# Two layers of memory attention and gMLP on one core: row norms and output splits moved to the end of each attention step, and the weights of the prologue staged and split another way

## The chip, the cores and the metric

The kernel runs on one core of a Trainium2 chip. The metric is the device time of one execution in microseconds; several executions are taken and their median is compared. A core has five engines that run side by side and meet only at semaphores: PE (TensorE, matmuls), DVE (VectorE), ACT (ScalarE), POOL (GpSimd) and SP (SyncE, which here only issues DMAs). Each works its own instruction list strictly in order, so an instruction that waits holds back everything behind it on its engine.

## The reference

`x` is 2048 rows of 640. All matrices and `x` are f32.

```
A(x):  q, k, v = x@wq, x@wk, x@wv      # 32 heads of 20, four segments of 512 rows
       for each segment s:
         a_dot = softmax(q k^T * scale + causal mask) v
         a_mem = phi(q) M / (phi(q) z + 1e-6)        # phi(t) = t+1 if t>0 else exp(t)
         o     = g * a_mem + (1-g) * a_dot           # g = sigmoid(beta), one per head
         M, z += phi(k)^T v, sum of phi(k)
       return o @ wo
B(x):  z = gelu(x @ w_in);  z1, z2 = halves of z;  z2 = layernorm(z2)
       return (z1 * (w_sp @ z2 + b_sp)) @ w_out      # w_in 640x1728, w_sp 2048x2048
x = x + A(LN(x));  x = x + B(LN(x));  x = x + A(LN(x));  x = x + B(LN(x))
```

## The kernel before

**Splits.** Every f32 operand of a matmul becomes a high and a low f16 part, and three products stand for one. The pattern "ACT rounds to the high part, DVE or POOL subtracts to get the low part" comes back everywhere: for weights it is `split_scaled` (L81 on ACT, L82 on DVE, after a power-of-two scale `iv` that needs the largest absolute value of the whole weight), for the normed rows `split_t` (L320 on ACT, L321 on POOL, then the transposing DMA L322 into `xt`), for the exponentials `cast` (`PH` on ACT, L1328, and `PL` on POOL, L1332, two halves of 640 columns per head).

**Stages of a layer.** Attention (`Attention.run`), then phase 1b (the input product of the gMLP, tile by tile of 128 rows in the order 0, 8, 1, 9, ...), then phase 2 (the spatial product and the output product). Layer 0 also has a prologue: `prologue` loads wv, takes its largest value and splits it; `early()` in `run` norms the first four row tiles, runs the value products (`value`, L1052, tile `vps`) and, in between, `query_key_weights` takes the maxima of wq and wk (L225) and splits them; then come the products of the first units (`unit`, L1111, `kps` and `qps`).

**Attention in steps.** 64 pairs of heads (16 in each segment) are worked in steps `t`, five steps for two pairs. In a step PE makes logits twice: by queries (`mp`, whose row maxima DVE takes, L1316 and L1319, `mxs`) and by keys (`es`, exponentiated by ACT into `P` or `Pb`, L1293). `cast` splits them, `pvs` (L1366) multiplies by the values, `combine` (L1377 to L1394) divides and gates on DVE and POOL into `gm`; when a unit of six or eight heads is full, its `out` splits `gm` into `ohl` (L1402 on ACT, L1403 on POOL) and stores it. `by_queries`, `by_keys`, `pvs` are the rigid skeleton. Between them PE does the dense work: values, keys and queries of the next segment, the memory update (`mup` on PE; L1215 on DVE masks it into `mst`, and on POOL L1217 adds the old memory), the memory read (`num`, L1180, reads `mst`) and for some tiles the output projection (`yps`, L1084).

`prep(t)` makes a row tile's norm in two parts: `stats` (L305 to L308: mean and variance on DVE, the power on POOL, `lnrs`) and `norm` (L1033 on DVE, then the split). Such side jobs are put off with `post(k, f)`: `f` runs `k` steps later, in the list `self.later`, right after the step's logits and ahead of its `pvs` and `cast`. `self.half` runs at 0.8 of the step.

**What sets the order.** PE's order in the attention is the order in which this program is written. The other engines' order is found by a scheduler from priorities (`tc.high_priority`) and from explicit edges (`tc.issue_after`). SP's DMA queue has one order too, also by that scheduler.

**Start of phase 1b.** `load(t)` brings the row tile (L359) that the attention's projection has stored (L1092, `x<-xt`); `attn_out` norms it (`layernorm_stats`, then L390 and L391); `xn_t` splits it on ACT (L400) and DVE and transposes it by a DMA into `th` (L402), which the first matmul of phase 1b (`zp`, L412) reads.

Of the kernel before, what the change touches and what calls it, by code (L numbers as in the profile page):

```python
# [33 lines left out]
HP = 2000  # L34
# [147 lines left out]
def prologue(g, ctx, wv, wq, wk, wo, w_in, w_out):  # L182
# [7 lines left out]
    with tc.tile_pool(name="wpro", bufs=1, side="right", reuse_waits="tile") as p, \  # L190
# [5 lines left out]
        with tc.high_priority(offset=HP):  # L196
            am = p.tile([128, KD], F32, name="wamk")
            for k in range(KD):
                nc.vector.tensor_reduce(am[:, k:k + 1], st[:, k], AX.X, ALU.max, apply_absolute_value=True)
            nc.vector.tensor_reduce(g.wam[:, 0:1], am, AX.X, ALU.max)  # L200
            g.vscale = pow2_scales(g, p, pp, "wsc", g.wam, 0, 1)
        g.w["v"] = [wp.tile([128, KD, D], F16, name=f"wv{x}") for x in "hl"]
        g.wqk = {nm + x: nc.dram_tensor(f"w_{nm}{x}", (128, KD, D), F16, kind="Internal").ap() for nm in "qk" for x in "hl"}
        for k in range(KD):
            e = split_scaled(g, g.w["v"][0][:, k], g.w["v"][1][:, k], st[:, k], 0)
            if k == 2:
                g.third = e
    g.qk_w = wq, wk


def query_key_weights(g, stage, pool, psum, tag):

    nc, tc = g.nc, g.tc
    st = []
    for w, x in zip(g.qk_w, "hl"):
        parts = [g.top[1].tile([128, 2160], F32, tag=f"wi1{x}", name=f"wst{x}1")[:, :3 * D].rearrange("p (k c) -> p k c", c=D),
                 g.top[0].tile([128, 1600], F32, tag=f"wo{x}", name=f"wst{x}2")[:, :2 * D].rearrange("p (k c) -> p k c", c=D)]
        st.append([parts[k // 3][:, k % 3] for k in range(KD)])
        for k in range(KD):
            nc.sync.dma_start(st[-1][k], w[k * 128:(k + 1) * 128, :])  # L220
    for i, nm in ((1, "q"), (2, "k")):
        with tc.issue_after(g.vscale.ins):
            am = pool.tile([128, KD], F32, tag="wamk", name="wamk")
            for k in range(KD):
                nc.vector.tensor_reduce(am[:, k:k + 1], st[i - 1][k], AX.X, ALU.max, apply_absolute_value=True)  # L225
# [6 lines left out]
        for k in range(KD):  # L232
            split_scaled(g, h[:, k], l[:, k], st[i - 1][k], i)
        yield

# [102 lines left out]
def phase1b(g, o_d, x, x1_d, z1_d, zh, zl):  # L338

    nc, tc = g.nc, g.tc  # L340
    with ExitStack() as ctx:
# [75 lines left out]
        g.loaded, g.gelu, g.lo = {}, {}, {}  # L417
# [33 lines left out]
        with tc.high_priority(offset=3 * HP2):  # L451
            a = load(0)
        with tc.high_priority(offset=HP2):
            xn = attn_out(0, *a)
            a = load(ORDER[1])
            th = xn_t(*xn)
        for i, t in enumerate(ORDER):
# [3 lines left out]
            if i + 1 < NT:  # L461
                xn = attn_out(ORDER[i + 1], *a)
# [402 lines left out]
def attn_consts(g, cp, beta):  # L865
# [6 lines left out]
    with tc.tile_pool(name="tmp", bufs=1) as tp, tc.tile_pool(name="acp", bufs=1, space=PSUM) as pp:  # L872
        f = tp.tile([128, 192], F32, name="fmask")
        for t, n, b, sg, op in ((g.eye, 64, 0, 1, ALU.not_equal), (g.step["q"], 192, -64, 1, ALU.is_ge), (g.step["k"], 192, 64, -1, ALU.is_ge)):
            nc.vector.memset(f, 0.0)
            for h in range(2):
                v = f[64 * h:64 * h + 64, :n]
                nc.gpsimd.affine_select(v, v, [[sg, n]], op, BIG if op is ALU.not_equal else -BIG, base=b, channel_multiplier=-sg)
            nc.vector.tensor_copy(t, f[:, :n])
# [7 lines left out]
        nc.vector.tensor_scalar(g.gate, g.gate, 1.0, 0.125, ALU.add, ALU.mult)  # L887

# [29 lines left out]
class Attention:  # L918
# [9 lines left out]
    def __init__(self, g, x, o_d, x1_d):  # L928
# [8 lines left out]
        self.now, self.later, self.half, self.rd = None, {}, {}, set()  # L937
        self.lead = []

    def post(self, k, f, c=None, into=None):  # L940
# [7 lines left out]
        (self.later if into is None else into).setdefault(t, []).append(f)  # L948
# [60 lines left out]
    def prep(self, t):  # L1009
# [4 lines left out]
        nc.sync.dma_start(xt, self.x[t])  # L1014
        ln = []

        def behind():
            ctx = ExitStack()
            for e in (g.hold[:2] or (g.third,)) if t > 1 else ():
# [11 lines left out]
        def last():  # L1031
            mv, rs = ln
            nc.vector.tensor_scalar(xt, xt, mv[:, 0:1], rs, ALU.subtract, ALU.mult)  # L1033
            hl = self.e2.tile([128, 2, D], F16, tag="xh", name="xnhl")
            e = split_t(g, hl, self.xt[s % 2][:, :, :, c], xt, low=nc.vector if g.hold and t in (2, 3) else nc.gpsimd)
            if t == 3:
# [4 lines left out]
    def value(self, t):  # L1041
# [5 lines left out]
        for n in range(2):  # L1047
# [8 lines left out]
            def out(ps=ps.rearrange("p (h d) -> p h d", d=DH), v=self.vs[s % 2][:, t % 4, n * 16:(n + 1) * 16, :]):  # L1056
                nc.scalar.mul(v[:, :, 0:DH], ps, QS)
                nc.vector.scalar_tensor_tensor(v[:, :, DH + 1:], ps, QS, v[:, :, 0:DH], ALU.mult, ALU.subtract)
# [38 lines left out]
    def unit(self, s, m):  # L1097
# [3 lines left out]
        for nm in "qk" if s else "kq":  # L1101
# [96 lines left out]
    def update(self, s, m):  # L1198
# [20 lines left out]
        self.post(1, out)  # L1219

    def stack(self, nm, s, m, hl):
# [6 lines left out]
        if nm == ("k" if s else "q"):  # L1228
# [93 lines left out]
    def cast(self, n, h):  # L1322
# [7 lines left out]
        def low(engine):  # L1330
            for c in (slice(0, 640), slice(640, 1280))[::-1 if n % 2 and h else 1]:
                engine.tensor_tensor(PL[:, c], P[:, h, c], PH[:, c], ALU.subtract)  # L1332
# [20 lines left out]
    def pvs(self, n, h, s, m, h0):  # L1353
        nc = self.nc
        PH, PL = self.P.pop((n, h))
        if h == 0:
            pv = self.po.tile([128, 512], F32, tag="pv", name="pv")
# [318 lines left out]
```

## Time and profile before

| | |
|---|---|
| median of 3 runs | 2218.08 us (2214.55 to 2218.99) |
| the profiled execution, its own time | 2217.2 us |
| its span | 2215.5 us |
| mean granted TensorE clock | 0.991 |
| busy: PE / DVE / ACT / POOL | 2087.8 / 1625.6 / 1250.9 / 1402.7 us |
| prologue (to the first `mp`) | 0 to 66.8 us |
| attention, layer 0, without its end | 66.8 to 575 us |
| end of that attention, to the first `zp` | 575 to 594 us |
| attention, layer 1, without its end | 1130 to 1660 us |
| end of that attention, to the first `zp` | 1660 to 1677 us |

The stage borders are the starts of the named tiles' first matmuls in the timeline, rounded. A row of a timeline reads: start, length, engine, line, operation, output<-inputs, count, and in brackets the idle time of that engine before the row with what ended it. "(x30)" behind a busy time is a number of instructions.

### The profile page before, as it was taken

Reading aid. Unit: us, or ns where it says so; the run is one execution under the profiler, and the core shown is the slowest. Engines: PE = TensorE matmul, PEld = TensorE weight load, DVE = VectorE, ACT = ScalarE, POOL = GpSimd, SP = SyncE. Lnnn points to the kernel's source line nnn. Section 1 sums busy time; section 2 is a strip of 40 time slices with the busy share of each in tenths; the row PEclk is TensorE's granted clock in tenths of the full one; section 3 lists DMA queues with packets and bytes.
Section 4 is the critical chain, followed back from the end, with each engine's and each line's share of the span. In section 5 each row is a group of like instructions: output and inputs, shape, how many; then the busy total and the mean of one; then the engine's idle time right before and its main releaser. Section 6 shows DMA issues by size and latency. Waiting matters only on the chain.

```text
span 2215.5 us, 53079 instructions
## 1 busy us (share of the span) xinstructions
PE 2087.8 (94%) x21322; PEld 1265.2 (57%) x21322; DVE 1625.6 (73%) x2889; ACT 1250.9 (56%) x1641; POOL 1402.7 (63%) x1172
## 2 busy tenths in 40 slices
PE   5998888999899999999999989989999999999999
PEld 3555655666545555555555556656665555555555
DVE  7788788788587758888657787787875764675563
ACT  4588788788644433333326987878884433333331
POOL 3387898788645345566414889888894433674660
PEclk9999999999999999999999999999999999999999
DMA  6666557344776686666455456553455335876752
GB/s 177 163 174 184 133 163 197 96 121 126 185 199 182 162 278 171 170 183 178 137 167 131 112 139 153 126 118 90 123 141 145 106 110 185 217 175 171 177 142 82
DMA packets 537703, 342.79 MB, mean 155 GB/s; under 512 B 411600, under 2 KB 463312, under 8 KB 537456
## 3 DMA queue, kind: packets, MB, share of 16 engines
q1 hardware_dynamic: 537456, 339.39, 57.2%
q8 instruction: 167, 2.74, 0.5%
q14 instruction: 80, 0.66, 0.1%
HBM read 159.18 MB, written 92.55 MB: 114 GB/s over the span
## 4 chain that ended last, share of the span: by engine, by line
PE 67%; DVE 14%; ACT 7%; issue 4%; DMA 4%; POOL 3%; SPq 1%; ACTq 0%; DVEq 0%; POOLq 0%
PE ga L670 12%; PE zp L412 11%; PE cyp L706 7%; PE pv L1366 4%; PE qps L1111 4%; PE vps L1052 3%; PE gb L670 3%; PE mp L1255 3%; PE yps L1084 3%; DVE mxs L1319 3%; PE gc L670 3%; PE gd L670 3%; PE kps L1111 2%; PE es L1255 2%; ACT PH L1328 2%
## 5 line engine op out<-in xcount | busy, mean ns | idle before, releaser
L1332 POOL TENSOR_TENSOR PL<-P,PH 128x640 f16<-128x640 f32 x384 | 535.1, 1422 | 86.7 <-PE pv L1366 67.9
L1319 DVE TENSOR_REDUCE mxs<-mp 128x2 f32<-128x1024 f32 (+2 forms) x384 | 320.2, 861 | 123.4 <-PE mp L1246 121.3
L1293 ACT ACTIVATE P<-es,sc 128x1024 f32<-128x1024 f32 (+1 forms) x256 | 271.6, 1061 | 102.0 <-PE es L1246 95.8
L640 POOL TENSOR_TENSOR ts<-ts,wt 128x512 f32<-128x512 f32 x196 | 283.3, 1457 | 11.0
L412 PEld LDWEIGHTS <-th 128*128 128x128 f16 x1920 | 188.0, 98 | 169.6 <-issue 6.9
L1328 ACT CAST PH<-P 128x1280 f16<-128x1280 f32 x192 | 239.7, 1249 | 2.5 <-PE pv L1366 1.0
L670 PEld LDWEIGHTS <-wts 128*128 128x128 f16 x1536 | 150.2, 98 | 134.0 <-issue 5.5
L670 PE MATMUL ga<-zh,wts 128*128 128x432 f16 x768 | 210.8, 346 | 4.5 <-ACT u L737 4.5
L308 POOL TENSOR_TENSOR lnrs<-lnve,mhalf 128x1 f32<-128x1 f32 x96 | 59.8, 631 | 230.2 <-DVE lnve L307 223.1
L1332 POOL TENSOR_TENSOR PL<-Pb,PH 128x640 f16<-128x640 f32 x124 | 175.8, 1447 | 20.3 <-PE pv L1366 19.3
L412 PE MATMUL zp<-wi,th 128*128 128x432 f16 x960 | 181.2, 346 | 3.5 <-ACT z L448 3.5
L640 POOL TENSOR_TENSOR ts<-wt,wt 128x512 f32<-128x512 f16 x28 | 33.9, 1211 | 226.3 <-DMA wt<-wn 226.3
L1052 PE MATMUL vps<-wvh,xt 128*128 128x320 f16 x640 | 154.8, 309 | 23.7 <-DVE relu L1143 13.0
L670 PEld LDWEIGHTS <-wt 128*128 128x128 f16 x1152 | 112.7, 98 | 96.5
L1366 PE MATMUL pv<-vs,PH 128*128 128x41 f16 x2560 | 158.6, 182 | 8.6 <-DVE gm L1387 5.5
L706 PE MATMUL cyp<-wuh,ut 128*128 128x320 f16 (+1 forms) x896 | 163.6, 299 | 2.7 <-DMA ut<-un 1.8
L706 PEld LDWEIGHTS <-ut 128*128 128x128 f16 (+1 forms) x1344 | 131.1, 98 | 57.5 <-DMA ut<-un 4.0
L1255 PEld LDWEIGHTS <-qk 64*128 64x128 f16 (+1 forms) x2048 | 77.9, 94 | 150.1 <-issue 129.3
L1366 PE MATMUL pv<-vs,PL 128*128 128x41 f16 x2560 | 156.3, 181 | 2.6 <-POOL PL L1332 2.6
L412 PE MATMUL zp<-wi1h,th 128*128 128x432 f16 x640 | 149.9, 349 | 2.2 <-DMA th<-xnhl 2.1
L524 DVE SCALAR_TENSOR_TENSOR wn<-wr,wsc,wn 128x512 f16<-128x512 f32 x126 | 92.9, 775 | 76.8 <-ACT wn L523 76.7
L1366 PEld LDWEIGHTS <-PH 128*128 128x128 f16 x2560 | 138.6, 96 | 15.2 <-ACT xnhl L400 2.9
(224 smaller groups left out, 5286.5 us busy)
## 6 DMA issues: line engine op xcount, KB each, us to landing
qk<-st SPq DMA_DIRECT2D x256, 120.0 KB
wr<-in_B_w_sp_dram SPq DMA_DIRECT2D x60, 512.0 KB
z<-z SPq DMA_DIRECT2D x32, 432.0 KB
cz<-z SPq DMA_DIRECT2D x32, 432.0 KB
xt<-in_A_x_dram SPq DMA_DIRECT2D x32, 320.0 KB
st<-khl SPq DMA_DIRECT2D x40, 256.0 KB
st<-qhl SPq DMA_DIRECT2D x40, 256.0 KB
x<-x SPq DMA_DIRECT2D x32, 320.0 KB
```

The costliest lines, as they stand in the source:

```text
L412: nc.tensor.matmul(zp[:, n, :FHH], a[:, k, :], b[:, k, c:c + FHH], start=(k == 0 and j == 0), stop=(k == KD - 1 and j == 2))
L640: nc.gpsimd.tensor_tensor(t, a, t if b == "t" else get(b), ALU.add if op == "+" else ALU.subtract)
L670: nc.tensor.matmul(ps, w[:, a, k % 4, :], z[:, k, j, :], start=start and k == 0 and i == 0, stop=k == NP - 1 and i == 2, skip_group_check= ...
L706: nc.tensor.matmul(yp[:, n, :320], a[:kn[k], k, :], b[:kn[k], k, n * 320:(n + 1) * 320], start=(k == 0 and j == 0), stop=(k == KO - 1 and ...
L1052: nc.tensor.matmul(ps, a[:, k, c], b[:, k, n * 320:(n + 1) * 320], start=(i == 0), stop=(i == 14))
L1111: nc.tensor.matmul(ps, a[:, k, c], b[:, k, :], start=(i == 0), stop=(i == 14))
L1255: nc.tensor.matmul(out[:, h, o:o + w], a[r, ac], b[r, bc], start=o == 0, stop=False, skip_group_check=True)
L1293: g.exp = nc.scalar.activation(P, E, AF.Exp, scale=g.esc)
L1319: e = nc.vector.tensor_reduce(mx[:, :, n, j], mp[:, :, o:o + w], AX.X, ALU.max)
L1328: nc.scalar.copy(PH, P[:, h])
L1332: engine.tensor_tensor(PL[:, c], P[:, h, c], PH[:, c], ALU.subtract)
L1366: nc.tensor.matmul(pv[:, i, h, :41], x[:, c:c + 128], v[:, j, h0 + h, :], start=(j == 0 and x is PH), stop=(j == i and x is PL), skip_grou ...
```

## The change

1. *Prologue, staging.* The raw rows of wq and wk are loaded into the tiles that will later hold the exponentials (`Pf`, `Pb`) instead of the top tiles. wq's five loads are issued behind the second row tile's load and ahead of the first transposing DMA; wk's five after the row tile of t=3, still ahead of the third and fourth transposing DMA.
2. *Prologue, splits.* wv is split in ten pieces of 320 columns, all of the first half's before the second's. The ten maxima of wq and wk are tied each to one eviction of a value product (`g.vlow`) and to the end of wv's split. Of wq and wk only columns 0 to 255 go through `split_scaled`; the other 384 columns are scaled on POOL (`tensor_scalar`), rounded on ACT and subtracted on POOL, ten times each. The key mask and the gate constants move behind wv's scale (`late_consts`). The first unit makes queries before keys.
3. *Steps.* `stats`, `norm` and `combine`'s `out` go to a new list `self.end`, run after all else of the step; the memory update's DVE part goes to the front of its step's list (`first=True`).
4. *End of an attention.* Of the last pair's `PL`, POOL makes the first half of each head and DVE the second (before: POOL one head, DVE the other, two steps later). The `pv` PSUM tile of two of the last three pairs comes from the pool `pm`. `combine`'s first operation of the last but one pair waits for the last `PL`. Phase 1b's loads of tiles 0 and 8 are made at its start with high priority, their norms tied behind two late `combine`s (`g.near`).

The core of the diff:

```diff
-        for k in range(KD):
-            e = split_scaled(g, g.w["v"][0][:, k], g.w["v"][1][:, k], st[:, k], 0)
+        for n in range(2):
+            c = slice(n * 320, (n + 1) * 320)
+            for k in range(KD):
+                e = split_scaled(g, g.w["v"][0][:, k, c], g.w["v"][1][:, k, c], st[:, k, c], 0)
...
+def load_rows(g, i):
+    for k in range(KD):
+        g.nc.sync.dma_start(g.qk_raw[i][k], g.qk_w[i][k * 128:(k + 1) * 128, :])
...
     for i, nm in ((1, "q"), (2, "k")):
-        with tc.issue_after(g.vscale.ins):
+        with tc.issue_after(g.split.ins), tc.issue_after(g.normed[i + 1].ins):
             am = pool.tile([128, KD], F32, tag="wamk", name="wamk")
             for k in range(KD):
-                nc.vector.tensor_reduce(am[:, k:k + 1], st[i - 1][k], AX.X, ALU.max, apply_absolute_value=True)
+                with tc.issue_after(g.vlow[(KD * (i - 1) + k) // 2].ins):
+                    g.kmax = nc.vector.tensor_reduce(am[:, k:k + 1], st[i - 1][k], AX.X, ALU.max, apply_absolute_value=True)
...
         for k in range(KD):
-            split_scaled(g, h[:, k], l[:, k], st[i - 1][k], i)
+            split_scaled(g, h[:, k, first], l[:, k, first], st[i - 1][k][:, first], i)
         yield
+    for i, nm in ((1, "q"), (2, "k")):
+        h, l = g.w[nm]
+        for k in range(KD):
+            w = st[i - 1][k][:, rest]
+            nc.gpsimd.tensor_scalar(w, w, g.iv[:, i:i + 1], None, ALU.mult)
+            nc.scalar.copy(h[:, k, rest], w)
+            nc.gpsimd.tensor_tensor(l[:, k, rest], w, h[:, k, rest], ALU.subtract)
...
-        for nm in "qk" if s else "kq":
+        for nm in "qk" if s or m == 0 else "kq":
...
-        self.post(1, out)
+        self.post(1, out, first=True)
...
-        self.post(2, out)
+        self.post(2, out, into=self.end)
...
                     for d, f in zip((2, 4), self.prep(i)):
-                        self.post(d, f)
+                        self.post(d, f, into=self.end)
...
             with self.behind(DVE):
                 until(t + 1)
+            with self.behind(DVE):
+                for f in self.end.pop(t, ()):
+                    f()
...
-        if h == 0 or n < self.N - self.TAIL:
-            low(nc.gpsimd)
-        else:
-            self.post(2, lambda: low(nc.vector))
+        for i, c in enumerate((slice(0, 640), slice(640, 1280))[::-1 if n % 2 and h else 1]):
+            self.low = (nc.vector if i and n >= self.N - self.TAIL else nc.gpsimd).tensor_tensor(PL[:, c], P[:, h, c], PH[:, c], ALU.subtract)
...
+            p, tag = (self.pm, "ms") if n in (self.N - 3, self.N - 1) else (self.po, "pv")
...
+        two = [pe2.tile([128, D], F32, tag="x1", name="x1") for _ in range(2)]
+        with tc.high_priority(offset=HP):
+            for t, x1 in zip(ORDER, two):
+                g.loaded[t] = nc.sync.dma_start(x1, x1_d[t])
...
         with tc.high_priority(offset=HP2):
-            xn = attn_out(0, *a)
-            a = load(ORDER[1])
+            with tc.issue_after(g.near[-4].ins):
+                xn = attn_out(0, two[0])
```

The order of the instructions moves at many places; three of them follow.

**DVE, prologue.** The stretch behind wv's split: `vs` is the eviction of a value product (PE's next one needs it done), `wamk` a maximum over one raw tile of wq or wk, `xt<-xt` a row norm. Before:

```order
L305 BN_STATS lnst<-xt 128x6 x2
L307 TENSOR_SCALAR lnve<-lnmv 128x1
L306 BN_AGGR lnmv<-lnst 128x2
L307 TENSOR_SCALAR lnve<-lnmv 128x1
L1058 SCALAR_TENSOR_TENSOR vs_297<-vps,vs_297 128x16x20
L1033 TENSOR_SCALAR xt<-xt,lnmv,lnrs 128x640 x2
L225 TENSOR_REDUCE wamk<-wsth_452 128x1 x3
L1058 SCALAR_TENSOR_TENSOR vs_297<-vps,vs_297 128x16x20
L225 TENSOR_REDUCE wamk<-wsth_453 128x1 x2
L1058 SCALAR_TENSOR_TENSOR vs_297<-vps,vs_297 128x16x20
L226 TENSOR_REDUCE wam<-wamk 128x1
L225 TENSOR_REDUCE wamk<-wstl_459 128x1 x3
```

and now:

```order
L1098 SCALAR_TENSOR_TENSOR vs_312<-vps,vs_312 128x16x20
L238 TENSOR_REDUCE wamk<-P 128x1 x2
L1071 TENSOR_SCALAR xt<-xt,lnmv,lnrs 128x640
L1098 SCALAR_TENSOR_TENSOR vs_312<-vps,vs_312 128x16x20
L238 TENSOR_REDUCE wamk<-P 128x1 x2
L1098 SCALAR_TENSOR_TENSOR vs_312<-vps,vs_312 128x16x20
L238 TENSOR_REDUCE wamk<-P 128x1
L239 TENSOR_REDUCE wam<-wamk 128x1
L238 TENSOR_REDUCE wamk<-P 128x1
L1098 SCALAR_TENSOR_TENSOR vs_312<-vps,vs_312 128x16x20
L238 TENSOR_REDUCE wamk<-P 128x1 x2
L62 TENSOR_REDUCE wmx<-wtp 1x1
```

The maxima now stand at most two between two evictions, where there were three or five.

**DVE, a step of the second segment with a memory update.** `mst<-mup` is the memory that PE's `num` waits for, `khl` the low part of the keys. Before:

```order
L1316 TENSOR_REDUCE mxs_304<-mp 128x2x2
L305 BN_STATS lnst<-xt 128x6 x2
L1129 SCALAR_TENSOR_TENSOR khl<-kps,khl 128x512
L1215 TENSOR_TENSOR mst_305<-mup,bmask 128x168
L306 BN_AGGR lnmv<-lnst 128x2
L307 TENSOR_SCALAR lnve<-lnmv 128x1
```

and now:

```order
L1356 TENSOR_REDUCE mxs_319<-mp 128x2x2
L1255 TENSOR_TENSOR mst_320<-mup,bmask 128x168
L1169 SCALAR_TENSOR_TENSOR khl<-kps,khl 128x512
L326 BN_STATS lnst<-xt 128x6 x2
L327 BN_AGGR lnmv<-lnst 128x2
L328 TENSOR_SCALAR lnve<-lnmv 128x1
```

The memory goes from behind the statistics and the keys to the front, and the statistics go behind the keys.

**SP, the end of layer 0's attention.** `x_..<-x_0_8` is the load of tile 8's stored rows (L359 before, L373 and L385 now), `wst` the raw weights of w_in, `th` phase 1b's transposed tile. Before:

```order
L129 DMA wst<-in_B_w_in_dram 128x864 x4
L1076 DMA xt<-in_A_x_dram 128x640
L359 DMA x_11495<-x_0_8 128x640
L1406 DMA o_3<-ohl 128x4x120
L359 DMA x_11563<-x_0_1 128x640
L1067 DMA_TRANSPOSE o<-o_2 128x10x128
L1406 DMA o_3<-ohl 128x4x120
L1092 DMA x_0_9<-xt 128x640
L1076 DMA xt<-in_A_x_dram 128x640
L359 DMA x_11637<-x_0_9 128x640
L1092 DMA x_0_10<-xt 128x640
L402 DMA_TRANSPOSE th<-xnhl 128x10x128
```

and now:

```order
L373 DMA x_11504<-x_0_8 128x640
L1385 DMA qk_308<-mr 2x4x128
L129 DMA wst<-in_B_w_in_dram 128x864 x4
L1116 DMA xt<-in_A_x_dram 128x640
L1442 DMA o_3<-ohl 128x4x120
L1107 DMA_TRANSPOSE o<-o_2 128x10x128
L1132 DMA x_0_9<-xt 128x640
L1442 DMA o_3<-ohl 128x4x120
L1116 DMA xt<-in_A_x_dram 128x640
L385 DMA x_11604<-x_0_1 128x640
L1132 DMA x_0_10<-xt 128x640
L385 DMA x_11678<-x_0_9 128x640
```

with `th`'s first transposing DMA next. Tile 8's load has moved ahead of the four loads of w_in; the loads of tiles 1 and 9, whose buffers are free only once ACT has read tiles 0 and 8, now stand closely ahead of `th`'s transposition.

More of the change, by code (lines that the diff above doesn't have):

```diff
@@ L887, in attn_consts @@
         nc.vector.tensor_scalar(g.gate, g.gate, 1.0, 0.125, ALU.add, ALU.mult)
+def attn_consts(g, cp):
+    nc, tc = g.nc, g.tc
+    g.eye = cp.tile([128, 64], F16, name="eye")
+    g.step = {nm: cp.tile([128, 192], F16, name="step" + nm) for nm in "qk"}
+    with tc.tile_pool(name="tmp", bufs=1) as tp, tc.tile_pool(name="acp", bufs=1, space=PSUM) as pp:
+        f = tp.tile([128, 192], F32, name="fmask")
+        for t, n, b, sg, op in ((g.eye, 64, 0, 1, ALU.not_equal), (g.step["q"], 192, -64, 1, ALU.is_ge)):
+            step_mask(g, f, t, n, b, sg, op)
         row = tp.tile([1, 3, 128], F32, name="mrow")
@@ L936, in __init__, with post @@
         self.mem, self.last, self.stacked, self.waiting = False, -1, -1, False
-        self.now, self.later, self.half, self.rd = None, {}, {}, set()
+        self.now, self.later, self.half, self.end, self.rd = None, {}, {}, {}, set()
         self.lead = []
-    def post(self, k, f, c=None, into=None):
+        g.near, g.normed, g.vlow = {}, {}, {}
+    def post(self, k, f, c=None, into=None, first=False):
         if self.now is None:
@@ L947, in post @@
             t += 1
-        (self.later if into is None else into).setdefault(t, []).append(f)
+        todo = (self.later if into is None else into).setdefault(t, [])
+        todo.insert(0 if first else len(todo), f)
     @contextmanager
@@ L1013, in prep @@
         xt = self.e2.tile([128, D], F32, tag="xt", name="xt")
-        nc.sync.dma_start(xt, self.x[t])
+        with self.tc.high_priority(offset=HP) if t in (2, 3) and not g.wo.made else ExitStack(), \
+                self.tc.issue_after(self.second.ins) if t == 3 and not g.wo.made else ExitStack():
+            self.row = nc.sync.dma_start(xt, self.x[t])
         ln = []
@@ L1434, in early @@
                     yield w
-                    if t > 1 and i in AT:
+                    if t == 2 and i in AT:
                         next(weights, None)
-            for _ in weights:
-                pass
-            yield from self.unit(0, 0)
+            next(weights, None)
+            for i, w in enumerate(self.unit(0, 0)):
+                yield w
+                if i == 6:
+                    next(weights, None)
+                elif i == 20:
+                    for _ in weights:
+                        pass
         rd = [(G * s + RD[m] + 5 * (c0 > 0), s, m, c0) for s in range(1, nseg) for m in range(NU) for c0 in range(0, len(UH[m]), 6)]
@@ L1595, in run @@
                 until(t + 1)
+            with self.behind(DVE):
+                for f in self.end.pop(t, ()):
+                    f()
         assert not self.half
-        for t in sorted(self.later):
-            self.now = None
-            for f in self.later[t]:
-                f()
+        self.now = None
+        for left in (self.later, self.end):
+            for t in sorted(left):
+                for f in left[t]:
+                    f()
 def phase1a(g, x, o_d, x1_d, nseg=NSEG):
```

80 lines of the change are left out of this document (44 added, 36 removed).

## The prediction

> **What bounds the kernel now.** I read the page's first and fourth parts, then the table by stage, then PE's waits in each, then the other engines' rows ahead of the longest.
>
> ```profile
> PE 2087.8 (94%) x21322; PEld 1265.2 (57%) x21322; DVE 1625.6 (73%) x2889; ACT 1250.9 (56%) x1641; POOL 1402.7 (63%) x1172
> PE 67%; DVE 14%; ACT 7%; issue 4%; DMA 4%; POOL 3%; SPq 1%; ACTq 0%; DVEq 0%; POOLq 0%
> ```
>
> The chain of waits is two thirds PE. PE is idle for 2215.5 − 2087.8 = 127.7 us; the change removes no matmul, so that is all there is to win. The stage table says where it lies (columns: stage, length, busy of PE, PEld, DVE, ACT, POOL, clock, DMA share, GB/s):
>
> ```profile
> 0.00:66.80 66.80, 43.60 (x221) 24.00 (x223) 48.10 (x132) 27.57 (x44) 16.89 (x37) 0.92 0.63 180
> 66.80:575.00 508.20, 465.51 (x7172) 300.88 (x7172) 416.40 (x802) 414.68 (x504) 416.84 (x345) 0.98 0.56 150
> 575.00:594.00 19.00, 11.89 (x188) 8.74 (x186) 8.38 (x22) 9.27 (x11) 12.14 (x10) 0.94 0.89 189
> 1130.00:1660.00 530.00, 497.26 (x7383) 319.98 (x7382) 404.06 (x784) 417.48 (x511) 414.51 (x350) 0.99 0.51 130
> 1660.00:1677.00 17.00, 12.92 (x208) 9.41 (x206) 8.35 (x22) 10.62 (x11) 13.04 (x11) 1.00 0.48 137
> ```
>
> PE stands idle 23.2 us in the prologue, 42.7 and 32.7 in the two attentions, 7.1 and 4.1 at their ends: 109.8 of the 127.7, all in the stages that the change touches. In the attentions DVE, ACT and POOL are each busy near 80%: an instruction moved there makes room for one and delays another.
>
> **Prologue, what leaves.** PE's three waits after its first value product, then what the products between them ran at:
>
> ```profile
> 31.65 0.31 PE L1052 MATMUL vps<-wvh,xt 128*128 128x320 f16 x1 [2.59 <-DMA xt<-xnhl]
> 45.84 1.03 PE L1111 MATMUL kps<-xt,wkh 128*128 128x512 f16 x2 [3.14 <-ACT wkh L81]
> 47.94 0.61 PE L1111 MATMUL kps<-xt,wkl 128*128 128x512 f16 x1 [1.07 <-DVE wkl L82]
> 45.80:56.50 10.70, 9.45 (x30) 0.69 0.29 95
> 56.50:63.40 6.90, 6.63 (x30) 1.00 0.57 153
> 18.72 3.31 SPq L220 DMA_DIRECT2D wsth<-in_A_wq_dram  x5
> 25.81 4.95 SPq L322 DMA_TRANSPOSE xt<-xnhl  x2
> 11.61 1.47 SPq L322 DMA_TRANSPOSE xt<-xnhl  x1
> 16.36 0.42 PE L1052 MATMUL vps<-wvh,xt 128*128 128x320 f16 x1 [2.02 <-ACT wvh L81]
> 16.40:31.60 15.20, 10.66 (x60) 6.25 (x59) 15.06 (x29) 5.90 (x10) 4.16 (x5) 1.00 0.96 292
> 24.15 2.26 DVE L225 TENSOR_REDUCE wamk<-wsth 128x1 f32<-128x640 f32 x3
> 40.95 3.69 ACT L81 ACTIVATE wqh<-wsth,iv 128x640 f16<-128x640 f32 x5
> 47.01 1.68 DVE L82 SCALAR_TENSOR_TENSOR wkl<-wstl,iv,wkh 128x640 f16<-128x640 f32 x2
> 40.78 1.40 POOL L321 TENSOR_TENSOR xnhl<-xt,xnhl 128x640 f16<-128x640 f32 x1 [0.42 <-ACT xnhl L320]
> ```
>
> The third transposition is issued at 25.8 behind both weights' loads and lands for 31.65; in the new order wq's loads are long done by then, so the 2.6 go. The first unit's 30 products (15 of keys, 15 of queries; 45.8 to 56.5) take 10.7 us at a granted clock of 0.69, the second unit's 30 take 6.9 at 1.00: the first are fed by split pieces of 0.84 us of DVE (1.68 / 2) and 0.74 of ACT (3.69 / 5). With 256 columns instead of 640 a piece costs 40% of that, 0.34, less than three matmuls (6.9 / 30 × 3 = 0.69): 3.8 go, the 1.07 among them, and the 3.14 ahead of them with the five wk pieces no longer queued behind five wq pieces. Together 2.6 + 3.8 + 3.1 = 9.5 us.
>
> *What comes.* Ten maxima at 0.75 (2.26 / 3) stay, two at most between two evictions: where PE needs the eviction for its next product, up to 1.5 us is late. The first transposition, issued at 11.6, now finds five more loads of 320 KB ahead of it; at the 292 GB/s of the full stretch above they take 5.5 us, begun about 4 and so nearly through: a delay between 0 and 5.5, of which the wait for wv's split (to 16.36) covers the first part. POOL gets 20 operations of 384 columns. No row shows one; 640 columns take 1.40 (above), so 0.84 by columns, 1.40 as the upper end: 17 to 28 us, on an engine that is idle after 42.2 before. They start with the scale at about 40 and are done by 57, or by 68; the third unit's products are the first to read these columns, and they come behind two units of 6.9 us and a value product from about 44 on, so from 61. By the nearer end the cover holds. I take 3.5 us back out of the 9.5: **−6 us**, ends −10 and +1.
>
> The Trainium skill (DMA: Bandwidth & Descriptors, Queues, rings and completion order) says that each DMA engine takes descriptors in ring order, which speaks against wq's loads ahead of the first transposition. The trace agrees in kind: the third transposition above took 5.8 us to land behind loads. By that rule 3.6 MB (wv, wq, a row tile) would be drained at 292 GB/s first, near 14 us, and the first product would start some 2 us late: −4 instead of −6.
>
> **Steps, what leaves.** The memory read `num` waits for the memory behind other DVE work:
>
> ```profile
> 207.91 0.46 PE L1180 MATMUL num<-mst,phq 128*128 128x126 f32 x2 [1.51 <-DVE lnmv L306]
> 206.06 0.88 DVE L305 BATCH_NORM_STATS2 lnst<-xt 128x6 f32<-128x320 f32 x2
> 206.85 0.68 DVE L1129 SCALAR_TENSOR_TENSOR khl<-kps,khl 128x512 f16<-128x512 f32 x1
> 207.44 0.32 DVE L1215 TENSOR_TENSOR mst<-mup,bmask 128x168 f32<-128x168 f32 x1
> 384.01 0.77 PE L1180 MATMUL num<-mst,phq 128*128 128x126 f32 x2 [2.65 <-DVE lnmv L306]
> PE num L1180 <- DVE lnmv L306: 4.2, 2, 2.7
> PE num L1180 <- DVE mst L1215: 2.8, 4, 1.2
> ```
>
> `lnmv` is named as releaser, but 4.2 + 2.8 = 7.0 us a layer is one wait, for `mst`; layer 1 has the same two rows with the same sums. With `mst` first, the row at 207.91 loses 0.88 + 0.68, capped at its 1.51; the one at 384.01 has the statistics and two more pieces ahead and I give it 2.0; the four others have at most one such piece ahead and lose some 0.15 each. That is 4.1 a layer, 8.2 in all. The second wait is longer:
>
> ```profile
> 231.05 0.43 PE L1052 MATMUL vps<-wvh,xt 128*128 128x320 f16 x1 [4.90 <-DVE relu L1143]
> 226.88 0.72 ACT L320 CAST xnhl<-xt 128x640 f16<-128x640 f32 x1 [0.89 <-DVE xt L1033]
> 229.00 0.71 ACT L1402 CAST ohl<-gm 128x640 f16<-128x640 f32 x1
> 229.61 0.66 ACT L1138 ACTIVATE kps<-kps,sc 128x512 f32<-128x512 f32 x1
> PE vps L1052 <- DVE relu L1143: 6.9, 2, 4.9
> ```
>
> PE's value product waits for DVE's `relu`, that for ACT's `kps`, and ahead of it ACT has a norm's and an output's cast: with both behind, 0.72 + 0.71 = 1.4 us go, and the norm on DVE ahead of the keys makes it 2.4 in layer 0; in layer 1, where the same line's waits are shorter, I take 1.0. So 11.6 us could leave the steps.
>
> *What comes.* All moved work still runs, in the same step or the next; a step lasts about 508 / 160 = 3.2 us, so nothing is over 3.2 us later. Late next are the transposed rows, the stored outputs, and `mxs`, DVE's maxima that PE's next logits wait for, which the moved pieces now stand close ahead of. With DVE at 82% I give back two fifths (11.6 × 0.6): **−7 us**, ends −12 and 0.
>
> **Ends of the attentions.** DVE sits at 575 for tile 8's rows, and what is behind it waits in turn; the last pair's `PL` on DVE (2.77 us at 587.95) keep its last multiplication and PE waiting:
>
> ```profile
> DVE lnst L305 <- DMA x<-x: 4.7, 1, 4.7
> 582.63 0.40 PE L1255 MATMUL es<-qk 64*128 64x384 f16 x4 [2.45 <-ACT Pb L1293]
> PE pv L1366 <- DVE gm L1387: 2.6, 1, 2.6
> 587.95 2.77 DVE L1332 TENSOR_TENSOR PL<-Pb,PH 128x640 f16<-128x640 f32 x2
> 584.12 2.09 SPq L402 DMA_TRANSPOSE th<-xnhl  x1
> 590.93 0.83 ACT L400 ACTIVATE xnhl<-xn,lnrs 128x640 f16<-128x640 f32 x1 [3.68 <-DMA th<-xnhl]
> ```
>
> Without the load's delay and with the second PSUM tile, PE's 2.45 and 2.6 go, 5.0 us of layer 0's 7.1. But `th`, which the next stage's first matmul reads, now stands in SP's queue behind the load of tile 9, which waits for ACT to have read tile 8 (after the last `PH`, some 1.5 us later than 584.12), and it took until 590.9 to land. So I keep half: −2.5, and −0.5 in layer 1, whose end has 4.1 us of idle: **−3 us**, ends −6 and 0. The order of PE's products within layer 0's phase 1b moves too, with the same products; PE is the engine it runs on without a break, so I cost it at nothing, with ±2 for the range.
>
> **Sum.** −6 − 7 − 3 = −16 against the profiled execution's 2217.2, whose span is 1.7 less and which stands 0.9 under the median: 2201.2, or 2202 against the median.
>
> **Rivals.** *A, the steps give all back.* What DVE and ACT do later in a step takes `mxs`' and `es`' time, as 80% busy engines would; then only prologue and ends gain, 2218 − 9 = 2209. For it: DVE is busy 416.4 of 508.2 us, so there are few holes to move work into. Against it: `num` and `relu` are single waits with the causes named.
>
> *B, POOL's pieces are slow.* At the 1.40 us of a 640-column piece, POOL ends at 68 while the third unit's low parts are wanted from 61 on: PE waits 7, the prologue gains nothing (−6 + 7), the time is 2218 − 9 = 2209. The Trainium skill (GPSIMD Engine Reference, Elementwise — side-by-side cycle accounting) gives 4497 ns for 2048 f32 columns of a two-input operation against DVE's 2293; that is 0.84 for 384, an estimate from that page, and by it the splits are done in time and the sum stays at 2202. No row of this trace has 384 columns.
>
> *C, outputs late, slower than before.* A unit's split now follows the step's work, and the projection reads all units of a segment. This row shows that one place has no slack:
>
> ```profile
> PE vps L1052 <- DMA o<-ohl: 1.3, 1, 1.3
> ```
>
> Each layer has four segments. If each now waits a full step, 3.2 us, 8 × 3.2 = 26 us come on top of −16: 2228. Slower from 2.6 us a place (8 × 2.6 = 21, past the 16 and the 0.2%). Against it: POOL's order keeps `ohl` within one pair of `PL` of its old place.
>
> *D, all of it.* Everything named leaves and nothing comes back: 9.5 + 11.6 + 5.5 = 27, so 2191. For it: no new wait is certain; against it: the three busy engines.
>
> **Chances.** My sum 0.50 (2195 to 2208), A 0.15, B 0.08, C 0.10, D 0.10; 0.07 for no change, if PE's idle time only moves. The range 2190 to 2216 leaves C and that case out. A run tells 0.2% (4.4 us) from no change: faster 0.81 (of A's and B's 0.23 a little falls within), same 0.09, slower 0.10.
>
> **What would show it.** Right: the first `mp` near 61 instead of 66.8; `num` without `lnmv` among its waits and under 3.5 us a layer; the wait at 231 under 3.5; DVE without the 4.7 for tile 8's rows, and layer 0's `zp` 2 to 3 us nearer to the last `mp`. Wrong: the third unit's `kps` or `qps` waiting for POOL (B); PE waiting for `o<-ohl` or `xt<-xnhl` in each segment (C); `mxs` and `P` waits that grow by what `num` lost (A); or `th` waited for at the stage's border for longer than PE's two waits there were.

## The result and the profile after

The changed kernel takes 2194.69 us (median of 6 runs, 2189.93 to 2202.12) against 2218.53 us of the kernel before, taken beside it: a ratio of 0.9895, 95% interval 0.9874 to 0.9915, or 24 us less. Its profiled execution has a span of 2193.2 us, 22.3 less than that of before. Below stand four stages that the change touches by the table of stages (columns as in the prediction; the borders are the first or last matmul of the named tiles: first `mp`, last `mp`, first `zp`), before:

```profile
0.00:66.74 66.74, 43.54 (x219) 23.94 (x220) 48.10 (x132) 27.57 (x44) 16.89 (x37) 0.92 0.63 180
66.74:560.81 494.07, 452.14 (x6940) 291.51 (x6941) 408.92 (x780) 402.62 (x491) 403.50 (x335) 0.98 0.56 149
560.81:593.63 32.82, 24.95 (x420) 18.01 (x417) 15.70 (x43) 21.17 (x22) 25.48 (x20) 0.97 0.84 193
1169.06:1647.30 478.24, 448.03 (x6937) 288.93 (x6938) 380.15 (x723) 393.54 (x476) 397.92 (x335) 0.99 0.49 123
```

and after, the page's line of busy times first:

```profile
PE 2080.3 (95%) x21322; PEld 1261.3 (58%) x21322; DVE 1622.8 (74%) x2894; ACT 1251.8 (57%) x1656; POOL 1425.6 (65%) x1192
```

```profile
0.00:64.64 64.64, 40.56 (x219) 23.07 (x220) 47.54 (x137) 29.39 (x59) 37.50 (x56) 0.97 0.66 183
64.64:550.60 485.96, 449.61 (x6941) 289.62 (x6941) 408.60 (x774) 400.73 (x490) 402.74 (x336) 0.99 0.57 152
550.60:582.00 31.40, 25.96 (x421) 18.42 (x417) 19.50 (x53) 22.60 (x24) 27.20 (x21) 0.95 0.79 199
1157.29:1625.54 468.25, 445.65 (x6938) 287.50 (x6939) 373.38 (x717) 391.52 (x474) 397.44 (x334) 1.00 0.49 125
```

| | before | after | difference | forecast |
|---|---|---|---|---|
| prologue | 66.7 | 64.6 | −2.1 | −6 |
| attention's steps, layer 0 and 1 | 494.1 + 478.2 | 486.0 + 468.3 | −18.1 | −7 |
| ends of the attentions, layer 0 and 1 | 32.8 + 29.3 | 31.4 + 29.5 | −1.2 | −3 |
| all else | 1114.3 | 1113.4 | −0.9 | 0 |
| span | 2215.5 | 2193.2 | −22.3 | −16 |

The steps gave more than twice what was forecast and the prologue a third of it. And PE's busy time fell by 2087.8 − 2080.3 = 7.5 us with the same 21322 matmuls: a third of the gain is not idle time at all. The granted clock says the same of the other executions: 0.993 to 0.998 in the changed kernel's six, 0.987 to 0.993 in the 37 of the kernel before that ran beside the experiments.

The waits of the steps that were named in the prediction (layer 0's steps, then the whole prologue; who waits, for whom, us, times, longest):

```profile
PE num L1220 <- DVE mst L1255: 2.7, 4, 0.8
PE mp L1295 <- DVE mxs L1359: 8.9, 12, 1.4
PE vps L1092 <- DVE relu L1183: 6.3, 3, 2.9
PE vps L1092 <- DMA xt<-xnhl: 7.7, 2, 7.5
```

`num` went from 7.0 to 2.7 us in each layer, with `lnmv` gone from its waits. The longest wait for `relu`, 4.9 us before, is 2.9. `mxs` grew a little, in layer 0 from 7.3. The last row is the prologue's: before, its wait for a transposed row tile was 2.6.

### The profile page after: what moved, and what is told of

The parts are those of the page before. It is cut to its first block, busy times and chain, and to the rows that moved or that the text cites. A ratio compares the mean times of both kernels' runs of the same rounds, so it can differ in the third digit from the quotient of the medians.

```text
span 2193.2 us, 53140 instructions
## 1 busy us (share of the span) xinstructions
PE 2080.3 (95%) x21322; PEld 1261.3 (58%) x21322; DVE 1622.8 (74%) x2894; ACT 1251.8 (57%) x1656; POOL 1425.6 (65%) x1192
## 4 chain that ended last, share of the span: by engine, by line
PE 70%; DVE 11%; ACT 7%; DMA 5%; POOL 3%; issue 3%; SPq 1%; ACTq 0%; DVEq 0%; POOLq 0%
PE zp L438 14%; PE ga L695 12%; PE cyp L731 7%; PE qps L1151 4%; PE pv L1401 4%; PE vps L1092 3%; PE yps L1124 3%; PE gb L695 3%; PE mp L1295 3%; PE gc L695 3%; PE gd L695 3%; DVE mxs L1359 2%; POOL PL L1371 2%; PE es L1295 2%; PE kps L1151 2%
## 5 line engine op out<-in xcount | busy, mean ns | idle before, releaser
L695 PEld LDWEIGHTS <-wts 128*128 128x128 f16 x1536 | 150.2, 98 | 134.0 <-issue 5.5
L673 DVE TENSOR_TENSOR wts<-ts,wts 128x512 f16<-128x512 f32 x112 | 134.0, 1231 | 17.3 <-ACT wts L672 16.5
```

Of the source, the lines that this page charges most:

```text
L673: nc.vector.tensor_tensor(w[:, 1], t, w[:, 0], ALU.subtract)
L695: nc.tensor.matmul(ps, w[:, a, k % 4, :], z[:, k, j, :], start=start and k == 0 and i == 0, stop=k == NP - 1 and i == 2, skip_group_check= ...
```

## The experiments

Ten kernels ran. A ratio is to the kernel before, run beside it; its median there was between 2218.5 and 2219.5 us. Where a difference of two or three us is below what the ratios tell, the profiled executions' stages are compared, and it is said so.

### The memory update first, alone

On the kernel before:

```diff
-        self.post(1, out)
+        self.post(1, out, first=True)
```

> The kernel before with one edit: the memory update's DVE part goes to the front of its step's list. Theory 1 (a wait is paid twice: PE's idle time, and a stretch of about 3.4 or 6.8 us right after it at half the TensorE clock): num's waits fall from 7.0 to about 2.7 us a layer, the half-clock stretches at 384 and 1465 us go with them, attention is 6 to 7 us shorter in each layer, about 2205 us in all. Theory 2 (waits alone): 4.3 us a layer, 2210 us, with the half-clock stretches where they were or no matter. Theory 3 (the gain of the steps comes from norms and outputs at the step's end): 3 us in all, 2215 us.

Measured: 2202.26 us, ratio 0.9917 (0.9899 to 0.9935), so about 18 of the 24 us from one edit. In the profiled execution layer 0's steps are 487.2 us (−6.9) and layer 1's 472.1 (−6.1). `num` falls by 4.3 us a layer as forecast. The total is what theory 1 gave, but only in part by its reasons. The half-clock stretches at 384 and 1465 us did go; two others of 3.4 us came, at 105.6 and 1228.6, the first behind no wait of even 1 us. So PE's busy time in the steps falls by 0.7 and 0.6 us only, and the clock pays little here. The rest is a second wait, `vps` for `relu`, 6.9 to 4.5 in layer 0 and 5.6 to 4.5 in layer 1. It is the place of the 4.90 us wait that the prediction showed; ACT and PE there now:

```profile
226.43 0.45 ACT L1058 ACTIVATE vs<-vps 128x320 f16<-128x320 f32 x1
226.76 0.65 ACT L1139 ACTIVATE kps<-kps,sc 128x512 f32<-128x512 f32 x1
227.33 0.72 ACT L320 CAST xnhl<-xt 128x640 f16<-128x640 f32 x1
227.94 0.73 ACT L1403 CAST ohl<-gm 128x640 f16<-128x640 f32 x1
228.19 0.30 PE L1053 MATMUL vps<-wvh,xt 128*128 128x320 f16 x1 [2.86 <-DVE relu L1144]
```

Before, ACT made the norm's and the output's casts ahead of `kps`; now behind. Nothing in the edit speaks of these instructions: the scheduler found another order for ACT as well, and one piece moved on DVE moved three on ACT. With that order the 4.90 became 2.86; no run here moves ACT's pieces alone.

### Norms and outputs at the step's end, and norms alone

On the kernel before, all of `prep`'s and `combine`'s late jobs in the end list; then the norms without the outputs:

```diff
-        self.post(2, out)
+        self.post(2, out, into=self.end)
...
-                        self.post(d, f)
+                        self.post(d, f, into=self.end)
```

> The kernel before with one edit: row norms and output splits run at the end of their step. Theory 1: the statistics no longer stand ahead of the memory, which takes about 0.9 us from each of the two long num waits of a layer; whether a half-clock stretch goes depends on whether the wait falls under what the clock bears: 2 to 4 us a layer, 2211 to 2214 us. Theory 2: 2 us a layer, 2214. Theory 3: 7 us a layer, about 2204.

> The kernel before with only the row norms (statistics and norm) run at the end of their step; output splits stay where they were. The kernel with both gained 8 us. Theory 1 (the norms stand ahead of what PE waits for: statistics ahead of the memory, norm ahead of the keys): nearly all of it, 2212. Theory 2 (the outputs' casts on ACT hold up the units, and o's transposition is in time): a third or less, 2217.

Measured: 2211.37 us, ratio 0.9958 (0.9944 to 0.9973), and with the norms alone 2211.66, ratio 0.9964 (0.9948 to 0.9980). The norms carry all that the times can tell apart. The steps are 3.8 and 3.6 us shorter in the first kernel's profile, theory 1's upper end, and theory 3 falls. But theory 1's reason covers only a part: `num` falls from 7.0 to 6.6 us in layer 0 and to 5.4 in layer 1, and layer 0's longest wait, 2.65 before, has grown:

```profile
379.09 0.77 PE L1180 MATMUL num<-mst,phq 128*128 128x126 f32 x2 [3.08 <-DVE mst L1215]
```

More is gained where `vps` waits: in layer 0 its two waits for `relu`, 4.90 and 2.02, are 2.51 and 1.65, and in layer 1 a wait of 2.2 for `qhl` is gone. PE's busy time in the steps falls by 0.6 in each layer. Together with the first experiment (6.9 + 3.8 and 6.1 + 3.6) this is 10.7 and 9.7 us a layer, against 8.1 and 10.0 of the changed kernel. In layer 1 the two parts add; in layer 0 they overlap, since the same two waits for `relu` fell by 2.4 us with the memory alone, by 2.8 with the norms and outputs alone and by 2.0 with both.

### The prologue alone

The changed kernel with parts 3 and 4 undone.

> The kernel before with the change's prologue alone. If the stages add: first mp at 64.6 us instead of 66.7, all later stages as in the kernel before, 2216 us (within 0.2% of it). If an earlier or later start of the attention moves its waits too: the stages behind differ by more than 1 us each.

Measured: 2218.27 us, ratio 0.9994 (0.9982 to 1.0007): no change that can be told. The first `mp` stands at 64.2 us, as expected, so 2.5 us were won at this point; in this execution the later stages have lost them again: from layer 0's first `zp` to layer 1's first `mp` it takes 3.7 us longer than before, and layer 1's steps 2.1, as the expectation's second case has it (PE busy 2088.1, 0.3 above before). The same prologue's length varies by a us or two between executions: in the four profiles here with the old one the first `mp` stands at 64.9 to 66.7 (mean 65.7), in the five with the changed kernel's own at 63.0 to 64.6 (mean 63.7). So it is worth 2 us at that place, and by the time of the whole not more than 4.

### wq's loads behind the first transposition

On the changed kernel (`opening` is the first transposing DMA):

```diff
-                        load_rows(self.g, 0)
+                        with self.tc.issue_after(self.opening.ins):
+                            load_rows(self.g, 0)
```

> The changed kernel, with wq's five loads issued after the first transposing DMA instead of ahead of it. Ring order theory (the first transposition lands late because it queues behind wq's loads): the first value product starts near 16.5 us instead of 20.7 and the first mp 3 to 4 us earlier: 2191 us. Rival (the prologue is bound by the sum of its transfers or by DVE's maxima, which now start later): the wait moves to the second or third transposition, or to wq's scale, and the first mp gains under 1 us: 2194 us.

Measured: 2197.37 us, ratio 0.9892 (0.9875 to 0.9910), the same as the changed kernel. The first `vps` starts at 16.23 instead of 20.70, so wq's loads were the cause, as the ring order theory says, and the rival holds for the rest: the first `mp` is at 64.54 against 64.64. These rows show the changed kernel, where the loads came first:

```profile
4.11 4.43 SPq L225 DMA_DIRECT2D P<-in_A_wq_dram  x5
10.51 1.40 POOL L342 TENSOR_TENSOR xnhl<-xt,xnhl 128x640 f16<-128x640 f32 x1 [1.62 <-ACT xnhl L341]
11.93 3.54 SPq L1052 DMA_DIRECT2D xt<-in_A_x_dram  x1
15.51 4.48 SPq L343 DMA_TRANSPOSE xt<-xnhl  x2
20.70 0.45 PE L1092 MATMUL vps<-wvh,xt 128*128 128x320 f16 x1 [7.54 <-DMA xt<-xnhl]
```

and these show this run, SP first, then PE's waits in the prologue:

```profile
11.65 0.34 SPq L1052 DMA_DIRECT2D xt<-in_A_x_dram  x1
12.03 2.08 SPq L343 DMA_TRANSPOSE xt<-xnhl  x1
PE vps L1094 <- DMA xt<-xnhl: 4.5, 3, 3.3
PE kps L1153 <- DVE wkl L82: 2.9, 3, 1.4
PE wbc L67 <- DVE wam L239: 2.4, 1, 2.4
```

Most of the delay stands ahead of the transposition's issue, not behind it. In the changed kernel its rows are ready at 11.91 (POOL's 10.51 + 1.40), but SP spends 3.54 us on issuing the row tile's load ahead of it, against 0.34 here, and so issues it at 15.51 instead of 12.03. From that issue to the first product it is 5.2 us there and 4.2 here.

The second and third transpositions take over part of the wait, and then the chain of wk's scale, whose DVE splits `wkl` begin at 47.45 us, 1.8 us sooner than in the changed kernel where the first product came 4.5 us sooner.

### wk's scale earlier as well

On that kernel, PE's transposition for wk's maximum inside the last value product, and the scale right behind it:

```diff
-                    if t == 2 and i in AT:
+                    if t == 2 and i in AT or t == 3 and i == 8:
                         next(weights, None)
...
-                if i == 6:
-                    next(weights, None)
-                elif i == 20:
+                if i == 20:
```

> The changed kernel with wq's loads after the first transposing DMA, as in the run before, and besides PE's transposition for wk's largest value at 40 us instead of behind all value products and wk's scale right behind them instead of within the first unit's queries. Theory (with the loads moved, the chain of wk's maximum, its scale and its splits ended last): wk's splits begin near 45 us instead of 48, kps waits under 1 us in all, first mp at 61 to 62: 2191. Rival (DVE's splits and evictions, or POOL's pieces, end last anyway): first mp at 64 and a new wait of the third unit's kps for POOL: 2195 or more.

Measured: 2192.70 us, ratio 0.9882 (0.9863 to 0.9900). wk's splits begin at 44.84 us, as expected. The first `mp` is at 62.55, 2.1 us ahead of the changed kernel's profile, 1.2 ahead of the mean of the five with its prologue, and short of the 61 to 62 expected; `kps` waits 1.5 us in all, where under 1 was expected, and no unit waits for POOL. The mechanism holds by the trace; the time against the changed kernel is within the intervals.

### The end's part undone

The changed kernel with the last pair's `PL`, the PSUM tile, the edge and the early loads as before.

> The changed kernel with part 4 undone (last pair's PL, the PSUM tile, the combine's edge, phase 1b's early loads as before). If the end's gain is what the changed kernel's trace shows against before (last mp to first zp 31.4 us against 32.8 in layer 0, 29.5 against 29.3 in layer 1): within 2 us of 2194.7, so 2196. If the ends gained the 3 us forecast, or the early loads also spare the stage behind: 2198 to 2200. If the waits of th that stand in phase 1b of the changed kernel (5.6 us) come from part 4: faster than the changed kernel, 2191.

Measured: 2200.96 us, ratio 0.9912 (0.9896 to 0.9929). Against 0.9895 for the changed kernel this is 4 us more with intervals that overlap. By its profile the stages themselves do not differ: last `mp` to first `zp` 31.3 and 29.4 us against 31.4 and 29.5. So part 4 gave nothing at the place that it edits. The stage behind layer 0's end, to layer 1's first `mp`, hints at a gain: 575.1 to 576.3 us in the six profiles with part 4, 575.4 to 579.1 in the six without, 578.1 in this one. In it `zp` waits 3.6 us for ACT's `z` here and not at all in the changed kernel, where it waits 5.6 instead of 1.5 us for `th`. Whether that is worth anything in the time stays open.

### Two moves in SP's queue at the end

On the changed kernel: the four loads of w_in behind the last transposition of outputs, tile 9's load behind `th`'s.

```diff
-        with tc.high_priority(offset=HP), tc.issue_after(g.turned.ins), tc.issue_after(g.exp.ins):
+        with tc.high_priority(offset=HP), tc.issue_after(g.turned.ins), tc.issue_after(g.exp.ins), tc.issue_after(g.ot.ins):
...
+                with tc.issue_after(g.th0.ins) if t == ORDER[3] else ExitStack():
                     g.loaded[t] = nc.sync.dma_start(x1, x1_d[t])
```

> The changed kernel with two moves in SP's queue at the end of the attention: the four loads of w_in (1.7 MB) behind the last transposition of stored outputs instead of ahead of the projection's row tile, and the load of tile 9 behind the first transposition for phase 1b. Theory (the end gained nothing because DVE's wait for tile 8's rows behind w_in, 4.7 us, only became a wait for the projection's rows behind w_in, 3.7 us): that wait falls under 1 us, ACT's and POOL's waits behind it go too, last mp to first zp in layer 0 is 28 to 29.5 us instead of 31.4: 2192. Rival (the end is bound by POOL's and DVE's PL pieces): last mp to first zp stays at 31, 2195.

Measured: 2193.25 us, ratio 0.9884 (0.9870 to 0.9899). In layer 0 the last `mp` to the first `zp` is 28.4 us (−3.0), in layer 1 28.7 (−0.7). The theory holds for that wait; a later row tile is still waited for, 1.26 us. The two moves were not run apart. The time is not to be told from the changed kernel's: in this execution the last stage, from layer 1's first `zp` on, is 3.1 us longer (2.7 in the next run's), and whether that is chance is open. First the changed kernel (SP's queue and DVE at the end of layer 0's attention), then this one:

```profile
558.51 1.85 SPq L129 DMA_DIRECT2D wst<-in_B_w_in_dram  x4
560.40 0.55 SPq L1116 DMA_DIRECT2D xt<-in_A_x_dram  x1
568.77 0.55 DVE L1130 SCALAR_TENSOR_TENSOR xt<-yps,sc,xt 128x320 f32<-128x320 f32 x1 [3.69 <-DMA xt<-in_A_x_dram]
577.39 0.32 SPq L385 DMA_DIRECT2D x<-x  x1
577.80 1.49 SPq L428 DMA_TRANSPOSE th<-xnhl  x1
```

```profile
557.63 0.39 SPq L1119 DMA_DIRECT2D xt<-in_A_x_dram  x1
561.38 2.87 SPq L129 DMA_DIRECT2D wst<-in_B_w_in_dram  x4
563.79 0.55 DVE L1133 SCALAR_TENSOR_TENSOR xt<-yps,sc,xt 128x320 f32<-128x320 f32 x1
571.74 2.89 SPq L429 DMA_TRANSPOSE th<-xnhl  x1
577.61 0.38 SPq L386 DMA_DIRECT2D x<-x  x1
```

The change had taken tile 8's load out from behind w_in's four loads, and the next load in the queue, the projection's row tile, took its place: DVE had it 8 us after its issue, and DVE stood 3.69 us where it had stood 4.74.

### All of it

The two prologue edits and the two moves together.

> The kernel with wq's loads after the first transposition and wk's scale earlier (2192.7 us), with the same two moves in SP's queue. If both add: first mp near 62.5, the end 2 to 3 us shorter in layer 0: 2190, the fastest here. If the end's moves do nothing: 2193.

Measured: 2192.88 us, ratio 0.9884 (0.9867 to 0.9900), span 2189.0, the shortest span of all; first `mp` at 62.92, layer 0's end 28.3 us. Both parts are in the trace; the median is not to be told from either alone.

### A stall added: what a wait costs

On the changed kernel DVE forms the masked memory nine times over, to the same values:

```diff
-            nc.vector.tensor_tensor(new, mp, g.bmask[:, m, :n].unsqueeze(2).to_broadcast((128, n, DH + 1)), ALU.mult)
+            for _ in range(9):
+                nc.vector.tensor_tensor(new, mp, g.bmask[:, m, :n].unsqueeze(2).to_broadcast((128, n, DH + 1)), ALU.mult)
```

> The changed kernel with DVE's memory product done nine times over instead of once (same values written), so that what waits for it waits some 2.2 us longer at each of 15 updates a layer. Theory 1 (a wait is paid twice, through the clock): PE's idle time grows by 15 to 30 us a layer, and PE's busy time too, by 0.4 to 0.5 us for each us that the clock is at half, with half-clock stretches right behind the longer waits. Rival (waits alone): PE's busy time stays at 2080 us within 1, the granted clock at 0.994.

Measured, one execution: 2328.92 us. The page's busy times, PE's two longest waits, and the core's span and mean granted clock:

```profile
PE 2126.2 (91%) x21322; PEld 1284.8 (55%) x21322; DVE 1687.7 (73%) x3134; ACT 1256.6 (54%) x1656; POOL 1424.5 (61%) x1192
```

```profile
PE num L1220 <- DVE mst L1256: 61.6, 14, 6.1
PE mtp L1379 <- DVE mst L1256: 39.6, 13, 5.7
```

```profile
core 0: 2327.2 us, clock 0.967
```

All PE waits that the profile lists add up to 195 us against 107 in the changed kernel, 88 more (44 a layer: more than expected, since `mtp` waits for the same instructions). PE's busy time is 45.9 us longer with the same 21322 matmuls, and the mean granted clock falls from 0.994 to 0.967. So a us that PE waited cost another 45.9 / 88 = 0.5 us of slower matmuls. Theory 1 holds; waits alone would have left 2080. That this one execution was slow for some other reason is unlikely: outside the prologue, the steps and the ends its two stages last 575.1 and 538.7 us, in the changed kernel 575.3 and 538.2.

## Why the prediction was right, and where its steps were off

The time fell in the range, half beyond the forecast gain, and the terms do not match one by one. That the sum came so near is partly luck: the steps were forecast 11 us too small, the prologue and the ends together 6 too large. Of the signs named for "right", `num` and the wait at 231 came true; the first `mp` stands at 64.6 instead of near 61, and layer 0's `zp` came 1.4 us nearer to the last `mp`, not 2 to 3.

**Steps, −7 against −18.1.** The memory's term held: 4.1 a layer forecast, 4.3 measured. So, nearly, did that of `relu`: 2.4 and 1.0 forecast, 2.0 (4.90 and 2.02 to 2.87 and 2.10) and 0.6 measured. The list of waits shows only 0.6 in layer 0, because a wait of 1.33 us that stood under the stored outputs before stands under `relu` now, at the same product (first row before, second after):

```profile
128.74 0.30 PE L1052 MATMUL vps<-wvh,xt 128*128 128x320 f16 x1 [1.33 <-DMA o<-ohl]
126.32 0.30 PE L1092 MATMUL vps<-wvh,xt 128*128 128x320 f16 x1 [1.33 <-DVE relu L1183]
```

Three things make up most of the rest. The step "With DVE at 82% I give back two fifths" failed: `mxs` took back 1.8 us in layer 0 and 0.4 in layer 1, not 4.6; why the moved pieces cost so little was not tested. A wait that the sum did not name went as well, 2.2 us for `qhl` in layer 1; it is gone with the norms alone too, and still there with the memory alone. And the sum had no term for the clock. Before, this stands around the long `num` wait of layer 0 (the table by stage, columns as above):

```profile
376.00:383.60 7.60, 4.02 (x51) 2.86 (x50) 5.46 (x14) 5.67 (x7) 6.68 (x5) 1.00 0.75 182
380.12:383.53 3.41, 1.24 (x27) 0.74 (x23) 2.97 (x5) 2.59 (x3) 2.56 (x2) 1.00 0.85 210
383.60:390.40 6.80, 6.39 (x52) 5.30 (x53) 2.61 (x8) 1.53 (x2) 1.70 (x3) 0.50 0.26 59
384.57 0.46 PE L1184 MATMUL num<-mst,phq 128*128 128x21 f32 x2
384.86 0.77 PE L1180 MATMUL num<-mst,phq 128*128 128x126 f32 x2
```

and after, at the same matmuls, this:

```profile
377.20:384.00 6.80, 6.35 (x107) 5.15 (x108) 6.59 (x15) 4.67 (x6) 5.19 (x5) 1.00 0.79 147
377.65 0.46 PE L1220 MATMUL num<-mst,phq 128*128 128x126 f32 x2 [0.80 <-DVE mst L1255]
377.95 0.30 PE L1224 MATMUL num<-mst,phq 128*128 128x21 f32 x2
```

In 6.8 us at a granted clock of 0.50 PE did 52 matmuls, at 1.00 it did 107; the same pair of products took 0.77 and 0.46. Up to the last matmul, the trace's record of the clock has 41.0 us of such halved stretches before and 23.9 after, each 3.4 or 6.8 long; before, eight of nine come at a wait of 2 to 5 us, after, three of six, the others at waits of 1.1 to 1.4. From 23.9 to the stalled kernel's 150.2, PE's busy time follows at 0.36 us for each (45.9 / 126.3). In the steps PE's busy time gives 2.5 + 2.4 of the 18.1 us. The Trainium skill (TensorE: Matmul & The Clock Gate, What's actually happening) has the clock halved after an idle window of about 3.4 us and released after a busy one. The lengths agree; but here the stretch begins at 383.5, while `num` still waits and 2.2 us into its 2.65, so a gap shorter than the window was enough.

The traces say more. In each, all stretches up to the last matmul begin and end on one grid of 3.41 us frames, such as the row 380.12:383.53 above, in which PE was busy 1.24 us. Cut into these frames, the twelve profiles have 7527 at full clock up to the last matmul. In 76 PE was busy for less than 0.42 of the frame, and every one was followed by a halved frame; in 7155 it was busy for 0.7 or more, and none was; of the 296 between, 22 were. So a wait of two us halves the clock only when enough of it falls into one frame, which fits that like waits are followed by a stretch in one execution and not in another: the 2.2 us for `qhl` were not in the kernel before, and were in the first experiment, at 1228.6.

**Prologue, −6 against −2.1.** Of the 9.5 us the third transposition's 2.6 went (two waits for transposed rows are left, 7.5 for the first and 0.2). The step that failed is the one on the first: "a delay between 0 and 5.5, of which the wait for wv's split (to 16.36) covers the first part". The first product came 4.3 us late, past all cover, mostly because SP issued the transposition late; the run with the loads moved confirms the cause (16.23 us). The prediction's sentence on the Trainium skill's ring order (DMA: Bandwidth & Descriptors, Queues, rings and completion order), which gave 2 us, was nearer than the sum, though it reckoned with a late landing and not with a late issue. The other failed step is the 3.8 us of the first unit: its 30 products took 44.49 to 54.1, 9.6 us, 1.1 less than before instead of 3.8. A part is that wk's scale comes late and its splits with it: with that scale moved, the 30 products take 8.6 us, in both runs that move it. And a piece of 256 columns took 0.42 us on ACT (1.69 / 4) and 0.50 on DVE (2.50 / 5), not 0.34. The 3.14 ahead of wk's split fell to 0.3, but PE now waits 3.0 for the scales' `wbc`, before 0.6.

**POOL's pieces (rival B).** The scaling came out at the upper end, the subtraction at the lower:

```profile
39.17 7.02 POOL L253 TENSOR_SCALAR P<-P,iv 128x384 f32<-128x384 f32 x5 [0.45 <-DVE iv L74]
47.51 2.65 POOL L255 TENSOR_TENSOR wql<-P,wqh 128x384 f16<-128x384 f32 x3
64.00 1.78 POOL L255 TENSOR_TENSOR wkl<-Pb,wkh 128x384 f16<-128x384 f32 x2 [2.08 <-ACT wkh L254]
67.76 0.61 PE L1151 MATMUL kps<-xt,wkh 128*128 128x512 f16 x2
```

The five in the first row take 1.40 us each on average (1.24 to 1.84 over all ten), and the two-input subtraction mostly 0.91; the last is done at 65.8, and the third unit's first product at 67.8 did not wait. The cover held by 2 us.

**Ends, −3 against −1.2.** That `th` would stand behind tile 9's load was right, and cost at most 1.0 us at the border: the first `zp`'s weight load waits 0.96 us for it, and not at all where tile 9's load stands behind `th`; but its matmul waits as well, 0.85 us and to the same moment, for DVE to read the last pair's `pv`. Of "PE's 2.45 and 2.6 go" the second held; the first fell only to 1.4, and the step "Without the load's delay" failed, since the delay passed to the next load. PE's idle time in layer 0's end fell by 2.4 us, but its busy time rose by 1.0, at a clock of 0.95 instead of 0.97.

**Rivals.** A and C did not happen: `mxs` took 2.2 us of 18, and the one wait for stored outputs is no longer than it was. The time lies nearer to D's 2191 than to the sum's 2202, but not by D's way: the prologue gave a fifth of its 9.5, the ends a fifth of their 5.5, and the clock what no case had.

## What to carry to other kernels

When a matmul engine is over 90% busy, look at the granted clock behind each wait of two us or more: in the stalled kernel, whose long waits were 3 to 6 us, they cost about one and a half times their length, and a shorter one costs more than itself only where it leaves too little work in one frame of the clock. When a load is moved out from behind a block of large ones, ask which load is next behind that block; moving the block itself, with one smaller move beside it, was what shortened the end. When a transfer lands late, look first at when it was issued. And where a scheduler orders the engines, compare its lists after each edit: here the largest part came from one piece moved to the front on one engine, and of its 13 us in the steps 3.5 stand at the waits for `relu`, ahead of the longest of which another engine's list had changed too. A wait that changes its name has not gone: compare it by its place.

## What the runs showed of the hardware

POOL's one-input product of 384 f32 columns by a scalar per row took 1.24 to 1.84 us, longer than the two-input subtraction of as many columns with a 16-bit result (mostly 0.91), and about as long as a two-input one of 640 columns in the prediction's row (1.40). SP took 3.54 us to issue one load behind five of wq's, and 0.34 where they came later. And a PE wait has a second price through the clock, 0.5 us for each us in the stalled kernel, which no list of waits shows: it stands in the busy time, and it falls due when PE is busy for less than about half of one 3.41 us frame.
